# Sigmoid attention and ReGLU: part of the first queries loaded behind the first weights, and batch 1 in six bursts

One core of one Trainium2 chip. The metric is the device time of one execution in microseconds (us). The granted TensorE clock, the share of its full clock that the chip let TensorE have over a run, was 0.99 to 1.00. In lines of a profile PE is TensorE (PEld its weight loads), DVE is VectorE, ACT is ScalarE and POOL is GpSimd; what stands in brackets is idle time before the line, and what ended it.

## The reference

```python
def _attn_ref(q, k, v):                    # q, k, v: (8, 12, 448, 64) float32
    scores = (1 / sqrt(64)) * q @ k.T - log(448)
    return sigmoid(scores) @ v
def _moe_ref(x, w_gate, w_val, w_out):     # x: (3584, 768), d_ff 1536
    return (maximum(x @ w_gate, 0) * (x @ w_val)) @ w_out
```

The attention output, heads side by side, is the feed-forward input. Each of the 8 batches is one block of 448 tokens.

## The kernel before

Batch 0 is the ramp: the loads arrive while TensorE works. Its twelve heads are three groups, its queries are cut after three of seven chunks, and each of the six "slots" is one group against one half of the queries: scores, sigmoid on ScalarE, and a value product ("pv"). A feed-forward unit (`ffn_mix("f")`) is one 128-column piece of gate and value products. GpSimd issues loads that cast float32 to float16 on the way.

```python
    KCUT, QCUT = 4, 3                      # (two lines in the source)
    # first keys and queries of group 0: uncast, from SyncE and ScalarE queues; cast on VectorE, ScalarE
    make_identity(nc, ident[:])
    ...
    load(0, 0, 1, "k", KCUT)
    load(0, 1, 2, "kq")
    load(0, 2, 3, "kq")
    load(0, 0, 1, "q", QCUT)
    load_v(0)
    ...
    load_gv(0, 2)                          # gate and value weights, columns in pieces of 128
    load_gv(2, 4)
    load_gv(4, 6)
    load(1, 0, 1, "kq")
    load_gv(6, 8)
    ...
    after = {                              # (slot, unit): what TensorE does behind this unit's scores
        ...
        (0, 3): lambda: pe_transposes(0, 1, 1),
        (1, 2): lambda: pe_transposes(0, 2, 1),
        ...
        (2, 2): slots[0].pv,
        (2, 3): slots[1].pv,
        (3, 1): slots[2].pv,
        (3, 3): lambda: ffn_mix("f"),
        (4, 0): lambda: ffn_mix("f"),
        (4, 1): slots[3].pv,
        (4, 2): lambda: ffn_mix("f"),
        (5, 0): lambda: ffn_mix("f"),
        (5, 1): slots[4].pv,
        (5, 3): lambda: ffn_mix("ff"),
    }
    ...                                    # then slots[5].pv(), "the last slot's product"
        cuts = (0, 4, 7, 11, 16, 21) if b == 1 else (0, 5, 8, 13, 16, 21)   # score units of a burst
        pv_at = {3: 0, 4: 1} if b == 1 else {0: -1, 2: 0, 4: 1}
        if b == 1:
            mix = ["f" * n for n in (3, 4, 3, 3, 2)]                        # units between bursts
```

Of the kernel before, what the change touches and what calls it, by code (L numbers as in the profile page):

```python
# [17 lines left out]
def kernel(  # L18
# [10 lines left out]
    nc = tc.nc  # L29

    B, H, S, D = q.shape
    DM, DF = moe_w_gate.shape
    NPAIR = H // 2
    NG = H // 4
    P = 128
    NCH = S // 64
# [3 lines left out]
    QCUT = 3  # L40
# [32 lines left out]
    def bank(name):  # L73
        return next_ring().tile([P, 512], FP32, tag="ring", name=name)

    def bank16(name):
        return next_ring().tile([P, 1024], FP16, tag="ring", name=name)
# [5 lines left out]
    def tiles_of(b):  # L83
        if b not in in_tiles:
            in_tiles[b] = tuple(
                inp.tile([P, NPAIR, NCH * D], FP16, tag=t, name=t) for t in ("k16", "q16", "v16")
            )
        return in_tiles[b]

    def rows_of(src, b):  # L90
        return src[b].rearrange("(x r) (t c) d -> (r t) x (c d)", r=2, c=NCH)

    def load(b, g0, g1, which, c0=0):
        for nm, t16, src in zip("kq", tiles_of(b), (k, q)):
            if nm in which:
                xs = slice(2 * g0, 2 * g1)
                nc.gpsimd.dma_start(t16[:, xs, c0 * D :], rows_of(src, b)[:, xs, c0 * D :])  # L97

    def load_v(b):
        v16 = tiles_of(b)[2]  # L100
        nc.gpsimd.dma_start(v16[:, 0::2, :], rows_of(v, b)[:, 0::2, :])  # L101
        for r in range(2):
            nc.gpsimd.dma_start(  # L103
                v16[64 - 64 * r : P - 64 * r, 1::2, :], rows_of(v, b)[64 * r : 64 * r + 64, 1::2, :]
            )


    KCUT = 4
# [5 lines left out]
        first32.append(t32)  # L114
    zeros = const.tile([P, S], FP16, name="zeros")
    nc.vector.memset(zeros[:], 0.0)
    ident = const.tile([P, P], FP16, name="ident")
    make_identity(nc, ident[:])
    gate = const.tile([P, 2], FP16, name="gate")
    nc.gpsimd.tensor_copy(gate[:], zeros[:, 0:2])  # L120
    load(0, 0, 1, "k", KCUT)
    load(0, 1, 2, "kq")
    load(0, 2, 3, "kq")
    load(0, 0, 1, "q", QCUT)
    load_v(0)

# [4 lines left out]
    def load_gv(f0, f1):  # L131
        fs = slice(f0 * P, f1 * P)
        nc.gpsimd.dma_start(wg[:, :, fs], moe_w_gate[:, fs].rearrange("(c p) f -> p c f", p=P))
        nc.gpsimd.dma_start(wv[:, :, fs], moe_w_val[:, fs].rearrange("(c p) f -> p c f", p=P))

    load_gv(0, 2)
    load_gv(2, 4)
    load_gv(4, 6)
    load(1, 0, 1, "kq")
    load_gv(6, 8)  # L140
    load(1, 1, 2, "kq")
    load_gv(8, 10)
    load(1, 2, 3, "kq")
    load_gv(10, 12)
    load_v(1)

    def load_o():
# [9 lines left out]
    def keep_warm(count):  # L157
        ps = bank("warm_ps")
        for _ in range(count):
            nc.tensor.matmul(ps[:, 0:S], zeros[:, 0:P], zeros[:], start=True, stop=True)  # L160
# [19 lines left out]
    def qkT_of(b, g):  # L180
        if (b, g) not in qkT_tiles:
            qkT_tiles[(b, g)] = qkTp.tile([P, TW, P], FP16, tag="qkT", name="qkT")
        return qkT_tiles[(b, g)]

    def pe_transposes(b, g, ti, c0=0, c1=NCH):
        t16 = in_tiles[b][ti]
        qkT = qkT_of(b, g)
        trt = bank16("trt")
        for c in range(c0, c1):
            for h in range(2):  # L190
                nc.tensor.transpose(  # L191
                    trt[64 * h : 64 * h + 64, c * P : (c + 1) * P],
                    t16[:, 2 * g + h, c * D : (c + 1) * D],
                    ident[:],
                )
        nc.vector.tensor_copy(  # L196
            qkT[:, ti * NCH + c0 : ti * NCH + c1, :].rearrange("p c x -> p (c x)"),
            trt[:, c0 * P : c1 * P],
        )

    def dma_transposes(b, g):
        k16, q16, _ = in_tiles[b]
        rel = relp.tile([P, TW, P], FP16, tag="rel", name="rel")
        for ti, t16 in enumerate((k16, q16)):
            nc.vector.tensor_copy(
                rel[:, ti * NCH : (ti + 1) * NCH, :].rearrange("p c (h d) -> p h c d", h=2),
                t16[:, 2 * g : 2 * g + 2, :].rearrange("p h (c d) -> p h c d", c=NCH),
            )
        nc.sync.dma_start_transpose(
            qkT_of(b, g)[:], rel[:].rearrange("p c x -> p (c x)")  # L210
        )
# [68 lines left out]
    def qk_unit(b, g, c):  # L280
        ps = [bank("qk_ps") for _ in range(2)]
        qk(qkT_tiles[(b, g)], c, 0, NCH, lambda hh: ps[hh][:, 0:S])
        PT = PTp.tile([P, 2, 512], FP16, tag="PT", name="PT")
        for hh in range(2):
            sigmoid(PT[:, hh, 0:S], ps[hh][:, 0:S])
        PT_tiles[(b, g, c)] = PT

    def pv_group(b, g):
        pv(b, g, 0, S, [PT_tiles.pop((b, g, c))[:, :, 0:S] for c in range(NCH)])
# [69 lines left out]
    def push_gv(b, q0, qn, fs, act_relu=True):  # L359
        for f in fs:  # L360
            gv_queue.append(lambda f=f: gv(b, q0, qn, f, act_relu))

    def push_first(half, fs, act_relu=True):
        c0, c1 = HALVES[half]
        push_gv(0, 64 * c0, 64 * (c1 - c0), fs, act_relu)
# [5 lines left out]
    def ffn_mix(kinds, hooks=()):  # L371
        hooks = list(hooks)
        for left in range(len(kinds), -1, -1):
            while hooks and hooks[0][0] >= left:
                hooks.pop(0)[1]()
            if left:
                (gv_queue if kinds[len(kinds) - left] == "f" else y_queue).popleft()()
# [5 lines left out]
    nc.vector.tensor_copy(k16[:, 0:2, 0 : KCUT * D], first32[0])  # L383
    nc.scalar.copy(q16[:, 0:2, 0 : QCUT * D], first32[1])
    pe_transposes(0, 0, 0, 0, KCUT)
    keep_warm(2)
    pe_transposes(0, 0, 1, 0, QCUT)
    keep_warm(2)
    slots = [FirstSlot(g, half) for half in range(2) for g in range(NG)]
    push_first(0, range(0, 6), False)  # L390

    after = {
        (0, 0): lambda: pe_transposes(0, 0, 0, KCUT, NCH),
        (0, 1): lambda: keep_warm(2),
        (0, 2): lambda: pe_transposes(0, 1, 0),
        (0, 3): lambda: pe_transposes(0, 1, 1),
        (1, 0): lambda: keep_warm(2),
        (1, 1): lambda: pe_transposes(0, 2, 0),
        (1, 2): lambda: pe_transposes(0, 2, 1),
        (1, 3): lambda: keep_warm(2),  # L400
        (2, 0): lambda: keep_warm(2),
        (2, 1): lambda: pe_transposes(0, 0, 1, QCUT, NCH),
        (2, 2): slots[0].pv,
        (2, 3): slots[1].pv,
        (3, 1): slots[2].pv,
        (3, 3): lambda: ffn_mix("f"),
        (4, 0): lambda: ffn_mix("f"),
        (4, 1): slots[3].pv,
        (4, 2): lambda: ffn_mix("f"),
        (5, 0): lambda: ffn_mix("f"),  # L410
        (5, 1): slots[4].pv,
        (5, 3): lambda: ffn_mix("ff"),
# [15 lines left out]
    def pv_finish(b):  # L428
        pv_group(b, NG - 1)
        push_gv(b, 0, S, range(NFC))  # L430
        if b % 2:
            push_down(b // 2, range(7))
# [8 lines left out]
    def both(b, g):  # L441
        pe_transposes(b, g, 0)
        pe_transposes(b, g, 1)
# [6 lines left out]

    ffn_mix("fff", [(1, lambda: both(1, 0))])
    for b in range(1, B):
        cuts = (0, 4, 7, 11, 16, 21) if b == 1 else (0, 5, 8, 13, 16, 21)
        pv_at = {3: 0, 4: 1} if b == 1 else {0: -1, 2: 0, 4: 1}
        hooks = {}
        if b == 1:
            mix = ["f" * n for n in (3, 4, 3, 3, 2)]
            hooks = {
                1: [(1, lambda: both(1, 1))],
                2: [(1, lambda: both(1, 2))],  # L460
                3: [(1, lambda: dma_transposes(2, 0))],
                4: [(1, late_loads)],
            }
        elif b == 2:
            mix = ["fff", "fff", "ffy", "fyf", "fyf"]
        elif b % 2:
            mix = ["fyf", "fyf", "ffff", "fyf", "fyf"]
        else:
            mix = ["fff", "fyf", "fyf", "fff", "fyf"]
        for m in range(5):  # L470
            for i, (g, c) in enumerate(order[cuts[m] : cuts[m + 1]]):
                if i == (1 if b == 1 else 2) and m in pv_at:
                    if m == 0:
                        pv_finish(b - 1)
                    else:
                        pv_group(b, pv_at[m])
                qk_unit(b, g, c)
            if m >= 3 and 1 < b < B - 1:
                dma_transposes(b + 1, m - 3)
            if m == 0 and b > 1:  # L480
                dma_transposes(b, 2)
            if b == 1:
                if m == 0:
                    load(2, 0, 1, "kq")
                    load(2, 1, 2, "kq")
                    load(2, 2, 3, "kq")
            elif m == 0 and b + 1 < B:
                if b == 2:
                    hold(2, 2)
                load(b + 1, 0, 3, "kq")  # L490
                load_v(b + 1)
            ffn_mix(mix[m], hooks.get(m, ()))
# [34 lines left out]
```

## Time and profile before

| | before |
|---|---|
| time | 432.81 us (432.5 to 433.04, 4 runs) |
| TensorE busy | 422.5 of 430.9 us |
| V of batch 0 first in full use | 16.11 us |
| last slot's value product starts | 30.55 us |
| from there to the first full-width unit (batch 1's stage) | 38.11 us |
| from there to the end | 362.24 us |

### The profile page before, as it was taken

What the parts mean: (1) busy time and instruction counts of PE and PEld (TensorE: products, weight loads), DVE (VectorE), ACT (ScalarE), POOL (GpSimd) and SP (SyncE); (2) the same over time, 40 slices, a digit from 0 to 9 for tenths busy, and PEclk for the clock granted to TensorE, in tenths of its full rate; (3) what the DMA queues carried; (4) which work ended last, traced back from release to release, by engine and by line L of the source; (5) the groups of instructions that cost most, each with busy time, mean ns of one, the idle gap of its engine ahead of it and who ended that gap; (6) DMA issues with size and microseconds to landing.
All of it is one profiled execution on the core that took longest, in us unless ns stands there. A gap on an engine that the chain in (4) does not pass through costs nothing.

```text
span 430.9 us, 8612 instructions
## 1 busy us (share of the span) xinstructions
PE 422.5 (98%) x3670; PEld 235.5 (55%) x3670; DVE 130.6 (30%) x248; ACT 211.3 (49%) x451; POOL 50.5 (12%) x75
## 2 busy tenths in 40 slices
PE   8899999999999999999999999999999999999996
PEld 3587865455555455455555555455555545555563
DVE  3353344323312333222331323322332222222111
ACT  4865686645555455454554545655653545122110
POOL 8544202500120002000030000100000000000000
PEclk9999999999999999999999999999999999999999
DMA  9999946999997134944289133611333101100234
GB/s 151 199 199 200 203 74 102 198 203 204 182 157 152 13 74 82 175 90 81 44 121 172 52 79 68 122 40 39 60 73 70 37 2 38 37 2 1 47 100 110
DMA packets 69830, 43.64 MB, mean 101 GB/s; under 512 B 35104, under 2 KB 66208, under 8 KB 69792
## 3 DMA queue, kind: packets, MB, share of 16 engines
q0 software_dynamic: 31776, 23.37, 37.0%
q1 hardware_dynamic: 37664, 19.47, 22.7%
q8 instruction: 28, 0.46, 0.4%
q10 hardware_dynamic: 352, 0.26, 0.2%
q14 instruction: 10, 0.08, 0.1%
HBM read 47.19 MB, written 11.01 MB: 135 GB/s over the span
## 4 chain that ended last, share of the span: by engine, by line
PE 94%; DMA 2%; POOL 1%; DVE 1%; ACT 1%; issue 0%; ACTq 0%; POOLq 0%
PE g_ps L297 26%; PE v_ps L297 25%; PE ya L335 17%; PE qk_ps L222 9%; PE yb L335 9%; PE pv_ps L240 7%; DMA v<-in_v_dram 2%; DVE xT L168 1%; PE trt L191 1%; POOL k L97 1%; ACT PT L177 1%; POOL q L97 0%; POOL v L101 0%; POOL v L103 0%; ACT ysb L349 0%
## 5 line engine op out<-in xcount | busy, mean ns | idle before, releaser
L177 ACT ACTIVATE PT<-qk_ps 128x448 f16<-128x448 f32 (+3 forms) x318 | 150.8, 592 | 36.0 <-PE qk_ps L222 36.0
L297 PE MATMUL g_ps<-xT,wg 128*128 128x448 f16 (+2 forms) x648 | 127.7, 332 | 0.3 <-DVE xT L168 0.2
L297 PE MATMUL v_ps<-xT,wv 128*128 128x448 f16 (+2 forms) x648 | 126.8, 332 | 0.0
L315 DVE TENSOR_TENSOR hT<-gate_sb,v_ps 128x448 f16<-128x448 f32 (+2 forms) x108 | 61.1, 569 | 196.1 <-PE v_ps L297 114.8
L335 PEld LDWEIGHTS <-hT 128*128 128x128 f16 x672 | 65.7, 98 | 47.0
L306 ACT ACTIVATE gate_sb<-g_ps 128x448 f32<-128x448 f32 (+2 forms) x102 | 54.4, 545 | 75.2 <-PE g_ps L297 73.2
L297 PEld LDWEIGHTS <-wv 128*128 128x128 f16 x648 | 62.5, 98 | 47.4 <-issue 0.7
L297 PEld LDWEIGHTS <-wg 128*128 128x128 f16 x648 | 59.1, 98 | 48.7 <-issue 10.0
L335 PE MATMUL ya<-wo,hT 128*128 128x512 f16 x336 | 77.1, 379 | 0.0
L349 ACT ACTIVATE ysb<-yb 128x256 f32<-128x256 f32 x28 | 10.8, 384 | 102.1 <-PE yb L335 102.1
L222 PE MATMUL qk_ps<-qkT 64*64 64x448 f16 (+2 forms) x756 | 51.8, 336 | 2.3 <-ACT PT L177 1.1
L335 PE MATMUL yb<-wo,hT 128*128 128x256 f16 x336 | 41.3, 273 | 0.0
L240 PE MATMUL pv_ps<-PT,v 64*64 64x448 f16 (+2 forms) x756 | 36.8, 329 | 0.6 <-DMA v<-in_v_dram 0.6
L222 PEld LDWEIGHTS <-qkT 64*64 64x64 f16 x756 | 20.6, 105 | 30.1 <-issue 21.5
L168 DVE TENSOR_SCALAR xT<-pv_ps 128x448 f16<-128x448 f32 (+2 forms) x54 | 28.4, 568 | 26.2 <-PE pv_ps L240 26.2
L343 DVE TENSOR_SCALAR ysb<-ya 128x512 f32<-128x512 f32 x28 | 19.4, 692 | 55.4 <-PE ya L335 55.4
L240 PEld LDWEIGHTS <-v 64*64 64x64 f16 x756 | 21.4, 107 | 11.8 <-DMA v<-in_v_dram 0.8
L101 POOL DMA_DIRECT2D v<-in_v_dram x8 | 6.0, 747 | 172.4 <-PE qk_ps L222 172.1
L97 POOL DMA_DIRECT2D q<-in_q_dram x14 | 10.6, 759 | 9.9 <-DMA wo<-in_moe_w_out_dram 5.9
L97 POOL DMA_DIRECT2D k<-in_k_dram x14 | 10.9, 777 | 6.2 <-PE v_ps L297 1.6
L103 POOL DMA_DIRECT2D v<-in_v_dram x16 | 10.1, 635 | 2.2 <-DMA wg<-in_moe_w_gate_dram 1.3
L196 DVE COPY qkT<-trt 128x896 f16<-128x896 f16 (+2 forms) x14 | 7.5, 556 | 6.6 <-PE trt L191 6.5
(25 smaller groups left out, 54.6 us busy)
## 6 DMA issues: line engine op xcount, KB each, us to landing
out_dram<-ysb SPq DMA_DIRECT2D x54, 192.0 KB, 2.7
k<-in_k_dram POOLq DMA_DIRECT2D x5, 672.0 KB, 14.2
q<-in_q_dram POOLq DMA_DIRECT2D x5, 672.0 KB, 18.0
v<-in_v_dram POOLq DMA_DIRECT2D x8, 336.0 KB, 4.9
v<-in_v_dram POOLq DMA_DIRECT2D x16, 168.0 KB, 5.6
wg<-in_moe_w_gate_dram POOLq DMA_DIRECT2D x6, 384.0 KB, 12.7
wv<-in_moe_w_val_dram POOLq DMA_DIRECT2D x6, 384.0 KB, 12.4
k<-in_k_dram POOLq DMA_DIRECT2D x8, 224.0 KB, 10.2
```

The lines of the kernel that those rows point to most:

```text
L97: nc.gpsimd.dma_start(t16[:, xs, c0 * D :], rows_of(src, b)[:, xs, c0 * D :])
L103: nc.gpsimd.dma_start(v16[64 - 64 * r : P - 64 * r, 1::2, :], rows_of(v, b)[64 * r : 64 * r + 64, 1::2, :])
L168: nc.vector.tensor_scalar(out=xT_of(b, pr)[:, q0 : q0 + qn], in0=src, scalar1=XSCALE, scalar2=None, op0=AOP.mult,)
L177: nc.scalar.activation(PT_ap, ps_ap, AF.Sigmoid, bias=sig_bias, scale=qk_scale)
L222: nc.tensor.matmul(out_of(hh)[o : o + 64, :], qkT[rows, c, cols], qkT[rows, NCH + c0 : NCH + c1, cols], start=True, stop=True, tile_positi ...
L240: nc.tensor.matmul(ps[hh][64 * r : 64 * r + 64, 0:qn], v16[rows, 2 * g + hh, c * D : (c + 1) * D], pieces[c][rows, hh, :], start=(c == 0), ...
L297: nc.tensor.matmul(ps[-1][:, 0:qn], wt[:, dc, f * P : (f + 1) * P], xT_tiles[(b, dc)][:, q0 : q0 + qn], start=(dc == 0), stop=(dc == NDC - 1),
L306: nc.scalar.activation(gate_sb[:, 0:qn], ps[0][:, 0:qn], AF.Relu)
L315: nc.vector.tensor_tensor(out=hT_tiles[(g, f)][:, o : o + qn], in0=gate_sb[:, 0:qn], in1=ps[1][:, 0:qn], op=AOP.mult,)
L335: nc.tensor.matmul(ps[:, 0 : m1 - m0], hT_tiles[(g, f)][:, t * P : (t + 1) * P], wo[:, f, m0:m1], start=(f == 0), stop=(f == NFC - 1),)
L343: nc.vector.tensor_scalar(out=ysb[:, m0:m1], in0=ps[:], scalar1=OUT_SCALE, scalar2=None, op0=AOP.mult)
L349: nc.scalar.activation(ysb[:, m0:m1], ps[:, 0 : m1 - m0], AF.Copy, scale=OUT_SCALE)
```

## The change

The intent: the second parts of groups 1 and 2's queries aren't needed until slots 4 and 5, so they are taken out of the queue ahead of V and put behind the first weights, to let V land sooner. The first casting load moves to the head of GpSimd's work. Batch 1's scores come in six bursts of three or four units rather than five of up to five, and the later weights in pieces of three.

```diff
-    nc.gpsimd.tensor_copy(gate[:], zeros[:, 0:2])
-    load(0, 0, 1, "k", KCUT)
-    load(0, 1, 2, "kq")
-    load(0, 2, 3, "kq")
+    load(0, 0, 1, "k", KCUT)              # now ahead of make_identity
+    for g in range(1, NG):
+        load(0, g, g + 1, "k")
+        load(0, g, g + 1, "q", 0, QCUT)   # 192 columns, 384 bytes as float16
     load(0, 0, 1, "q", QCUT)
     load_v(0)
 ...
     load_gv(0, 2)
+    load(0, 1, NG, "q", QCUT)             # the query rest: 256 columns, 512 bytes
     load_gv(2, 4)
     load_gv(4, 6)
     load(1, 0, 1, "kq")
-    load_gv(6, 8)
+    load_gv(6, 9)
     load(1, 1, 2, "kq")
-    load_gv(8, 10)
+    load_gv(9, 12)
     load(1, 2, 3, "kq")
-    load_gv(10, 12)
     load_v(1)
 ...
-    keep_warm(2)                          # between the first two transposes
+    def second_queries():
+        pe_transposes(0, 1, 1, QCUT, NCH)
+        ffn_mix("f")
+        pe_transposes(0, 2, 1, QCUT, NCH)
 ...
-        (0, 3): lambda: pe_transposes(0, 1, 1),
+        (0, 3): lambda: pe_transposes(0, 1, 1, 0, QCUT),
-        (1, 2): lambda: pe_transposes(0, 2, 1),
+        (1, 2): lambda: pe_transposes(0, 2, 1, 0, QCUT),
-        (3, 3): lambda: ffn_mix("f"),
-        (4, 0): lambda: ffn_mix("f"),
+        (3, 2): lambda: ffn_mix("f"),
+        (3, 3): second_queries,
-        (4, 2): lambda: ffn_mix("f"),
+        (4, 3): lambda: ffn_mix("f"),
 ...
-        cuts = (0, 4, 7, 11, 16, 21) if b == 1 else ...
-        pv_at = {3: 0, 4: 1} if b == 1 else ...
-            mix = ["f" * n for n in (3, 4, 3, 3, 2)]
+        cuts = (0, 3, 6, 9, 13, 17, 21) if b == 1 else ...
+        pv_at = {3: 0, 5: 1} if b == 1 else ...
+            mix = ["f" * n for n in (3, 3, 3, 2, 2, 2)]
```

The transposes and loads hooked into batch 1 move with its bursts (cut here).

More of the change, by code (lines that the diff above doesn't have):

```diff
@@ L91, in rows_of, with load @@
         return src[b].rearrange("(x r) (t c) d -> (r t) x (c d)", r=2, c=NCH)
-    def load(b, g0, g1, which, c0=0):
+    def load(b, g0, g1, which, c0=0, c1=NCH):
         for nm, t16, src in zip("kq", tiles_of(b), (k, q)):
             if nm in which:
-                xs = slice(2 * g0, 2 * g1)
-                nc.gpsimd.dma_start(t16[:, xs, c0 * D :], rows_of(src, b)[:, xs, c0 * D :])
+                xs, cs = slice(2 * g0, 2 * g1), slice(c0 * D, c1 * D)
+                nc.gpsimd.dma_start(t16[:, xs, cs], rows_of(src, b)[:, xs, cs])
     def load_v(b):
@@ L452 @@
     for b in range(1, B):
-        cuts = (0, 4, 7, 11, 16, 21) if b == 1 else (0, 5, 8, 13, 16, 21)
-        pv_at = {3: 0, 4: 1} if b == 1 else {0: -1, 2: 0, 4: 1}
+        cuts = (0, 3, 6, 9, 13, 17, 21) if b == 1 else (0, 5, 8, 13, 16, 21)
+        pv_at = {3: 0, 5: 1} if b == 1 else {0: -1, 2: 0, 4: 1}
         hooks = {}
         if b == 1:
-            mix = ["f" * n for n in (3, 4, 3, 3, 2)]
+            mix = ["f" * n for n in (3, 3, 3, 2, 2, 2)]
             hooks = {
                 1: [(1, lambda: both(1, 1))],
-                2: [(1, lambda: both(1, 2))],
-                3: [(1, lambda: dma_transposes(2, 0))],
-                4: [(1, late_loads)],
+                3: [(1, lambda: both(1, 2))],
+                4: [(1, lambda: dma_transposes(2, 0))],
+                5: [(1, late_loads)],
             }
@@ L469 @@
             mix = ["fff", "fyf", "fyf", "fff", "fyf"]
-        for m in range(5):
+        for m in range(len(mix)):
             for i, (g, c) in enumerate(order[cuts[m] : cuts[m + 1]]):
-                if i == (1 if b == 1 else 2) and m in pv_at:
+                if i == 2 and m in pv_at:
                     if m == 0:
```

## The prediction

> **What bounds the kernel now.** I read the page's busy shares first, then the table of busy time by stretch, then the timeline of TensorE and of GpSimd for the first 60 us, the chain that ended last, and last the DMA view cut into short windows.
>
> ```profile
> PE 422.5 (98%) x3670; PEld 235.5 (55%) x3670; DVE 130.6 (30%) x248; ACT 211.3 (49%) x451; POOL 50.5 (12%) x75
> ```
>
> ```profile
> 0.00:20.00 20.00, 16.56 (x302) 8.88 (x302) 6.83 (x16) 12.30 (x18) 14.81 (x26) 1.00 1.14 174
> 20.00:36.00 16.00, 15.73 (x274) 12.85 (x271) 8.23 (x22) 9.01 (x12) 7.07 (x10) 1.00 1.40 198
> 36.00:70.00 34.00, 33.48 (x441) 24.71 (x439) 13.50 (x33) 27.14 (x67) 5.91 (x9) 1.00 0.90 136
> 70.00:430.90 360.90, 356.69 (x2662) 189.02 (x2660) 102.03 (x178) 162.81 (x357) 22.71 (x32) 1.00 0.51 90
> ```
>
> In the second fence the columns after the stretch and its length are the busy time of TensorE, its weight loads, VectorE, ScalarE and GpSimd, then the granted clock, the DMA share and GB/s. TensorE is the bound: from 70 us on the change touches nothing, and of the 70 us before, TensorE is idle 3.4 + 0.3 + 0.5 = 4.2 us. A part of its busy time there is filler (the warm-up matmuls; 22 of them, about 0.19 us each, so 4 us). So nothing in this change can be worth 2% (8.7 us): the question is one of a microsecond or two. The place where it is decided is the wait for V:
>
> ```profile
> 7.30 8.77 DMA v<-in_v_dram
> ...
> 16.11 0.76 PE pv_ps L240 x25
> ```
>
> ```profile
> 16.11 0.76 PE L240 MATMUL pv_ps<-PT,v 64*64 64x192 f16 x25 [0.64 <-DMA v<-in_v_dram]
> ...
> 18.93 0.41 PE L222 MATMUL qk_ps<-qkT 64*64 64x256 f16 x8 [0.39 <-ACT PT L177]
> ...
> 28.23 0.30 PE L222 MATMUL qk_ps<-qkT 64*64 64x256 f16 x4 [0.20 <-ACT PT L177]
> ```
>
> The chain of the end runs back through TensorE without a hole to 16.11 us, and there goes over into the last piece of V landing at 16.07. Only small waits for ScalarE follow. Whatever moves that landing, or puts a new wait after it, moves the end of the kernel one for one.
>
> **What the loads do.** From 2 us to 53 us the DMA never rests, so landing times follow from what stands ahead in the queue. GpSimd allows 8 loads in flight: each issue waits for the eighth before it, so its waits tell landings: V's first piece 14.0, V 16.07, the first gate weights 17.6, the first value weights 19.6, the second pair 21.6 and 23.6, the third 25.6 and 27.6.
>
> ```profile
> 14.06 0.82 POOL L134 DMA_DIRECT2D wv<-in_moe_w_val_dram  x1 [1.16 <-DMA v<-in_v_dram]
> 17.69 0.84 POOL L133 DMA_DIRECT2D wg<-in_moe_w_gate_dram  x1 [0.61 <-DMA wg<-in_moe_w_gate_dram]
> 19.68 0.82 POOL L134 DMA_DIRECT2D wv<-in_moe_w_val_dram  x1 [1.15 <-DMA wv<-in_moe_w_val_dram]
> ```
>
> What matters most is the rate by size of piece. These are the DMA view's lines for 4.0 to 4.4, 8 to 9, and 17 to 18 us:
>
> ```profile
> DMA packets 57, 0.02 MB, mean 58 GB/s; under 512 B 53, under 2 KB 57, under 8 KB 57
> ...
> DMA packets 227, 0.19 MB, mean 190 GB/s; under 512 B 15, under 2 KB 227, under 8 KB 227
> ...
> DMA packets 392, 0.20 MB, mean 197 GB/s; under 512 B 8, under 2 KB 392, under 8 KB 392
> ```
>
> At 8 us full query rows move (448 fp16, 896 bytes written): 16 engines / 227 a us = 71 ns each. At 17 us weights move (512 bytes): 41 ns each, the same 200 GB/s. At 4 us the only load in the queue is the second part of the first keys, whose pieces are 192 fp16 = 384 bytes: 16 x 400 / 57 = 112 ns each. So a 384-byte piece takes longer than an 896-byte one.
>
> **What the Trainium skill says.** "DMA: Bandwidth & Descriptors", section Specifications, gives 512 B as the smallest transfer for line rate, below which the engine does a read-modify-write. The trace agrees in direction: 58 GB/s at 384 bytes, 197 at 512. The same page, section Queues, rings and completion order, says that an engine takes turns between the queues it has work for, a packet at a time; the trace fits, since the rate at 2.8 to 3.3 us is shared by the two uncast loads. Its section Anatomy of one DMA gives about 2.0 us of fixed cost, mostly the receipt. Counting bytes at the measured rates, V's data is through at about 14.1 us and lands at 16.07, which agrees, though slow engines may be part of it.
>
> **The change, part by part.**
>
> Query loads of groups 1 and 2. The full loads (224 KB each, 1.15 us at 200 GB/s) ahead of V become 96 KB each in 384-byte pieces; the 256 KB that remain (512-byte pieces, 1.3 us) go behind the first weight pair. By bytes alone V would land 256 KB / 200 GB/s = 1.3 us sooner. By the measured piece time, each of the two takes 256 pieces x 112 ns / 16 = 1.8 us, so 0.65 us more than the full row did: V lands 1.3 us later for this part. The pieces after the rest of the queries land 1.3 + 1.3 = 2.6 us later.
>
> Casting load issued first. The second part of the first keys is issued at about 0.74 us instead of 1.49. The engines are busy with the two uncast loads until 3.7 us, so the gain is what the small pieces can use beside them, an estimate of 0.5 us. The uncast keys, now sharing each engine, land perhaps 0.5 us later than 4.04; TensorE starts later but was to wait for V at 15.07 anyway (three of V's matmuls start there), so this costs nothing at the end.
>
> So V lands at about 16.07 + 1.3 - 0.5 = 16.9, the first value weights at 20.4, the rest of the queries at 21.7, the second and third weight pairs 2.1 us later than before (25.7, 29.7).
>
> TensorE after V. Before V one pair of warm-up matmuls and 16 transposes go: free, there it waits. After V those 16 transposes come back: 2 x 0.34 us (8 take 0.34 in the timeline at 14.54), beside which the 0.42 us copies on VectorE hide behind the first feed-forward unit. From V on: value products and scores of group 2 and slot 3 at ScalarE's pace (four sigmoids of 1024 columns, 3.35 us) bring the first feed-forward unit, now one step earlier in the order, to 19.7; its value half waits to 20.4. The transposes at 21.1 wait to 21.7. Slot 4 starts at 23.45 against 21.18, with one unit (1.02 us) already done. It then has less TensorE work between its sigmoids, which costs 0.4 us of waits. The value product of the last slot, at 30.55 now, comes at 30.55 + 2.27 - 1.02 + 0.4 = 32.2: **1.65 us later**.
>
> Batch 1 in six bursts and larger weight pieces. A burst of four score units is 16 matmuls in 1.03 us; a change of kind costs about 0.1 us on each side, so one more burst costs 0.2 us. The waits that it can remove are those at 54 to 64 us: 0.03 + 0.16 + 0.33 = 0.5 us idle; I take 0.3 of it. The larger pieces change no bytes; the first of them lands 2 us later in itself, and the weights concerned have some 8 us (34.7 landed, 42.58 used). V of batch 1, about 50.5 landed and 53.91 used, is called 1.4 us sooner in the order: its slack of 3.4 falls to 3.4 - 2.1 + 1.65 - 1.4 = 1.5, enough. Net -0.1 us.
>
> Sum: +1.65 - 0.1 = +1.5 us, so **434.1 us** if small pieces cost what the one load showed.
>
> **Rivals.** First, that the 112 ns are a matter of the first casting load, not of its size: it is the only one of its kind, and the queue was just starting. For: the DMA share was under one packet an engine then, and 1.25 to 1.45 later, when packets overlap. Against: the rate is level from 3.9 to 4.7 us, and the loads behind it reach full rate while GpSimd is still issuing. Then V lands at 16.07 - 1.3 - 0.6 = 14.1, TensorE gets there at about 14, and the wait for V turns into a wait for the rest of the queries (19.0) and for ScalarE: the last slot's product comes at about 29.3, **1.2 us sooner**, and the time is 431.3. Second, that the early casting load delays the first uncast keys much more, by a microsecond, and the first slots' sigmoids (2.6 to 2.8 us a slot on ScalarE) become the bound in place of V: TensorE is then ready at about 16, still no later than V. That makes 434 to 434.5. Third, that V of batch 1 or the late weights become a new wait at 50 to 54 us: the slack above speaks against it; if the loads are later than I reckon, up to 1 us more, 435.
>
> **Range and chances.** I give the small-piece account 0.65, the first rival 0.35; 0.65 x 434.1 + 0.35 x 431.3 = 433.1. I predict 433.2, and a range from just under the first rival to the third: 430.7 to 435.2. The part touched is 70 us, of which 4.2 are idle, so a gain of 8.7 us is out of reach, and a loss of 8.7 would need a stall that nothing shows: faster by over 2% 0.01, within 2% 0.97, slower 0.02.
>
> **What would show it.** The DMA view of the changed kernel between 5 and 11 us should have two stretches near 60 GB/s with most packets under 512 B. The wait of the first value product for V should end near 16.9 (14.1 for the rival), and slot 4's first scores start near 23.4 (20.6 for the rival), with TensorE waiting for the query rest ahead of them. Waits for ScalarE in slots 4 and 5 should grow by some 0.4 us. From 70 us on, every interval should be as before, shifted by one amount. A full rate with small pieces, or an idle stretch of over a microsecond in batch 1, would prove me wrong.

## The result

433.42 us (432.83 to 433.62, 4 runs) against 432.81: a ratio of 1.0012, 95% interval 0.9995 to 1.003. Ratios here are the mean time of one kernel's fast runs over that of the other's of the same rounds, so not quite the ratio of the medians. The time was predicted to 0.2 us. That it came so close is luck: 433.2 is, to 0.1, the mean of two accounts, 434.1 and 431.3, weighted by their chances, and neither came true. The profile shows that the way there was another.

The changed kernel's page and its busy time by stretch (columns as in the prediction):

```profile
PE 423.0 (98%) x3668; PEld 235.5 (55%) x3668; DVE 130.7 (30%) x250; ACT 211.2 (49%) x451; POOL 49.5 (11%) x73
```

```profile
0.00:20.00 20.00, 17.29 (x305) 9.79 (x306) 6.55 (x18) 13.21 (x19) 15.33 (x26) 1.00 1.16 173
20.00:36.00 16.00, 15.18 (x267) 12.15 (x266) 8.34 (x22) 8.01 (x11) 5.83 (x8) 1.00 1.36 200
36.00:70.00 34.00, 33.69 (x440) 24.39 (x439) 13.64 (x33) 27.11 (x66) 5.60 (x8) 1.00 0.88 135
```

TensorE's first 20 us are 0.7 us fuller than before (17.29 against 16.56), as if something had been won; the next 16 us are 0.55 us emptier (15.18 against 15.73). This is TensorE's timeline of the changed kernel (start, length, what, count, idle time before it):

```profile
14.08 1.06 PE L240 MATMUL pv_ps<-PT,v 64*64 64x192 f16 x28
...
14.98 0.66 PE L240 MATMUL pv_ps<-PT,v 64*64 64x192 f16 x23
16.20 0.32 PE L240 MATMUL pv_ps<-PT,v 64*64 64x192 f16 x5 [0.56 <-issue]
...
18.27 0.67 PE L297 MATMUL g_ps<-xT,wg 128*128 128x192 f16 x6
...
19.60 0.41 PE L191 MATMUL trt<-ident,q 128*64 128x128 f16 x8
...
21.38 0.63 PE L222 MATMUL qk_ps<-qkT 64*64 64x256 f16 x16
...
23.90 0.30 PE L222 MATMUL qk_ps<-qkT 64*64 64x256 f16 x4 [0.50 <-ACT PT L177]
...
30.59 0.96 PE L240 MATMUL pv_ps<-PT,v 64*64 64x256 f16 x28
```

V was in use from 14.1 us and, by the chain of waits, complete by 14.4 (the fourth matmul of the product starts at 14.38), not at the predicted 16.9: 1.7 us sooner than before. The first feed-forward unit started at 18.27 us against 20.08. And yet the last slot's product came at 30.59 against 30.55. V's gain had gone within 16 us. This profile is of the fastest of the four runs (432.83 us); a second profile of the same kernel, below, is closer to the median. The dead stop of 0.56 us within the second value product waits for nothing that the profile shows, and its cause stays open. The traces hold a lead that no run tested. In all five profiles in which TensorE is early at this product (both of the changed kernel, and later rest_later, rest_first and rest_first_reordered) it halts before the same matmul, the 24th of 28, and goes on 1.4 to 1.7 us after the end of one 16 KB packet of the DMA queue that the trace calls "instruction" (here the packet moves from 13.37 to 14.54 us). In the other eight it gets to that matmul 1.76 us or more after that packet, and does not halt. So TensorE may have been waiting for its next instructions.

The same read of the DMA as in the prediction, here from 6.2 to 6.6 us of the changed kernel, where the 384-byte pieces of group 1's queries move:

```profile
DMA packets 155, 0.06 MB, mean 153 GB/s; under 512 B 144, under 2 KB 155, under 8 KB 155
```

155 packets in 0.4 us are 16 x 400 / 155 = 41 ns each on 16 engines, where the prediction had 112. The trace also has each packet's own duration: in both kernels the median 384-byte packet takes 51 ns, the 512-byte one 60 and the 896-byte one 88. Packets overlap (the engines' share in that stretch is 147% by the same view), so 41 ns apart and 51 ns long do not clash.

### The profile page after: what moved, and what is told of

The parts are those of the page before. It is cut to its first block, busy times and chain, and to the rows that moved or that the text cites. A ratio compares the mean times of both kernels' runs of the same rounds, so it can differ in the third digit from the quotient of the medians.

```text
span 431.1 us, 8609 instructions
## 1 busy us (share of the span) xinstructions
PE 423.0 (98%) x3668; PEld 235.5 (55%) x3668; DVE 130.7 (30%) x250; ACT 211.2 (49%) x451; POOL 49.5 (11%) x73
## 4 chain that ended last, share of the span: by engine, by line
PE 95%; ACT 2%; DMA 1%; DVE 1%; issue 1%; ACTq 0%
PE g_ps L297 26%; PE v_ps L297 25%; PE ya L335 17%; PE qk_ps L222 10%; PE yb L335 9%; PE pv_ps L240 7%; ACT PT L177 1%; PE trt L191 1%; PE warm_ps L160 1%; DMA qkT<-rel 1%; DVE xT L168 0%; DVE qkT L196 0%; ACT ysb L349 0%; DVE zeros L116 0%; ACTq L177 0%
## 5 line engine op out<-in xcount | busy, mean ns | idle before, releaser
L222 PEld LDWEIGHTS <-qkT 64*64 64x64 f16 x756 | 20.5, 105 | 29.1 <-issue 20.7
```

Of the source, the lines that this page charges most:

```text
L222: nc.tensor.matmul(out_of(hh)[o : o + 64, :], qkT[rows, c, cols], qkT[rows, NCH + c0 : NCH + c1, cols], start=True, stop=True, tile_positi ...
```

## The experiments

Marks of all profiles, in us. "V" is when the bulk of the first value product starts, "rest" when the transposes of the query rest start, "last" when the last slot's product starts, "batch 1" from there to the first full-width unit. The median of the kernel before, on the same chip in the same rounds, stands in brackets. Each row's marks are those of one profile. batch1_only and cast_on_act have batch 0's loads as before, so their V and "last" show how far the old marks vary: by some 0.1 us.

| kernel | V | rest | last | batch 1 | time (before) |
|---|---|---|---|---|---|
| before | 16.11 | - | 30.55 | 38.11 | 432.81 |
| changed, first profile | 14.4 | 19.60 | 30.59 | 38.23 | 433.42 (432.81) |
| after_again | 14.76 | 20.33 | 31.32 | 38.24 | 433.21 (432.39) |
| loads_only | 15.60 | 20.46 | 31.44 | 38.11 | 433.27 (432.74) |
| batch1_only | 16.13 | - | 30.58 | 38.25 | 432.74 (432.74) |
| f1_late | 15.37 | 20.00 | 30.67 | 38.25 | 433.08 (432.74) |
| f1_late_b1old | 14.83 | 19.73 | 30.39 | 38.11 | 432.55 (432.74) |
| split_inplace | 16.00 | - | 30.62 | 38.10 | 432.96 (432.39) |
| early_only | 15.74 | - | 30.37 | 38.11 | 433.00 (432.39) |
| cast_on_act | 16.23 | - | 30.68 | 38.11 | 433.35 (432.39) |
| rest_later | 14.58 | 23.93 | 36.30 | 38.11 | 438.83 (432.71) |
| rest_first | 14.39 | 20.59 | 31.58 | 38.11 | 433.65 (432.71) |
| rest_first_reordered | 14.68 | 18.00 | 30.45 | 38.11 | 432.17 (432.71) |

In all thirteen profiles the time from the first full-width unit to the end is 362.2 to 362.3 us: nothing after 70 us plays a part. The 95% intervals of the times are some 0.12 to 0.18% wide on each side, 0.5 to 0.8 us, so steps under that size are read from the marks, not from the times.

### The first part alone: loads_only

```diff
 (the changed kernel, with the batch 1 plan and the weight pieces of before)
```

> The first part alone: the loads, transposes and order of batch 0 as in the changed kernel; batch 1 in five bursts and weights in pieces of two as before. Theory S (V lands 1.7 us sooner, but ScalarE stands idle for 1.5 us ahead of slot 4 because two feed-forward units come first, and then sets the pace): the last slot's value product again near 30.6 us, the kernel within 0.3 us of before. Rival B (the first part is a real gain and the six bursts take it back): 1 us or more faster than before. The small-piece account of the prediction: V after 16.5 us and the kernel 1.6 us slower.

433.27 us, ratio 1.0013 (1.0001 to 1.0025). V came 0.5 us sooner than before, not the 1.7 of the first profile, and the last slot's product 0.9 us later. So rival B, a gain in batch 0 that the bursts take back, falls: the first part alone is no gain. Theory S, as put, expected 30.6 and got 31.44: it lacks something. The line that names it, from TensorE's timeline of this kernel:

```profile
15.60 0.76 PE L241 MATMUL pv_ps<-PT,v 64*64 64x192 f16 x25 [1.11 <-DMA v<-in_v_dram]
...
20.46 0.41 PE L192 MATMUL trt<-ident,q 128*64 128x128 f16 x8 [0.29 <-DMA q<-in_q_dram]
```

TensorE waits twice now: 1.11 us for V, and then for the query rest.

### The second part alone: batch1_only

```diff
 (the kernel before, with the changed batch 1 plan and weight pieces)
```

> The second part alone: batch 0 as before, batch 1 in six bursts and the larger later weight pieces. Theory S: within 0.3 us of before, or up to 0.6 us slower, if the 0.6 us that the changed kernel's median lies over before comes from here. Rival B: 1 us or more slower than before.

432.74 us, ratio 1.0007 (0.9993 to 1.0021). The marks say it more finely: batch 1 takes 38.23 to 38.25 us in all four kernels with six bursts and 38.10 or 38.11 in all nine with five. The sixth burst with its weight pieces costs 0.13 us, and gives nothing.

### One feed-forward unit moved: f1_late and f1_late_b1old

```diff
-        pe_transposes(0, 1, 1, QCUT, NCH); ffn_mix("f"); pe_transposes(0, 2, 1, QCUT, NCH)
+        pe_transposes(0, 1, 1, QCUT, NCH); pe_transposes(0, 2, 1, QCUT, NCH)
+        (4, 0): lambda: ffn_mix("f"),
```

> The changed kernel with one move: the second feed-forward unit goes from ahead of slot 4's scores to behind their first unit, both query transposes directly one after the other. Theory S: slot 4's first sigmoid starts near 21.0 us in place of 21.9, ScalarE's idle time ahead of it falls from 1.5 to about 0.6 us, the last slot's value product comes 0.7 to 1.0 us sooner (29.6 to 29.9), and the kernel is as much faster than the changed one. Rival B or a bound by weights landing: no change within 0.3 us; if the second weight pair is late (23.7 us) it costs nothing here, since the unit that reads it stays where it is.

> The same move with batch 1 and the weight pieces as before the change. Theory S: the last slot's value product as in f1_late (29.6 to 29.9) and the kernel 0.7 to 1.2 us faster than before, so about 431.6. Rival B: slower in batch 0 is not the matter, this is then also no faster than loads_only.

433.08 us (ratio 1.0010, 0.9998 to 1.0022) and 432.55 us (0.9999, 0.9986 to 1.0012). ScalarE's idle time ahead of slot 4 fell to 0.81 and 1.08 us, from 1.53 in the first profile, 1.89 in loads_only and 2.03 in after_again. From the start of the rest's transposes to the last slot's product it is 10.67 and 10.66 us, where the changed order takes 10.99, 10.99 and 10.98 (changed, after_again, loads_only). So the order ahead of slot 4 is worth 0.33 us: ScalarE's pace is part of the loss, a third to a half of what I expected. Otherwise it is a matter of when V and the rest land: in f1_late TensorE waits 1.27 us for V and then for no load, in f1_late_b1old 0.72 us for V and 0.33 for the rest. These are f1_late's lines:

```profile
15.37 0.76 PE L240 MATMUL pv_ps<-PT,v 64*64 64x192 f16 x25 [1.27 <-DMA v<-in_v_dram]
...
20.00 0.64 PE L191 MATMUL trt<-ident,q 128*64 128x128 f16 x16
```

### Small pieces by themselves: split_inplace

```diff
-    load(0, 1, 2, "kq")
-    load(0, 2, 3, "kq")
+    for g in range(1, NG):
+        load(0, g, g + 1, "k")
+        load(0, g, g + 1, "q", 0, QCUT)
+        load(0, g, g + 1, "q", QCUT)
```

> The kernel before, with only the full query loads of groups 1 and 2 each cut into a 384-byte and a 512-byte piece at the same place of the queue: same bytes, same order, no other change. The prediction's account (112 ns a small piece): each cut load takes 1.8 + 0.66 us in place of 1.15, so V's bytes are through 2.6 us later (16.7 us against 14.1) and V lands near 18.5. Theory S (a small piece is busy 51 ns and engines overlap them, some 46 ns apart): each takes 0.74 + 0.66 us, V's bytes are through about 0.5 us later (14.6) and the kernel is about 0.5 us slower.

Counting the queue's bytes in order by the packet sizes in the trace, V's were through at 14.45 us, against 14.16 and 14.07 in the two profiles of the uncut queue (before and batch1_only). That count is rough, since the engines run out of step: V's own last packet started at 15.17, against 14.95 and 15.40. V was in use at 16.00, against 16.11 and 16.13. The account of 112 ns a piece (16.7 and 18.5 us) is wrong by a wide margin. The cost is at most the expected half microsecond.

### The early casting load: early_only

```diff
+    load(0, 0, 1, "k", KCUT)
     ident = const.tile([P, P], FP16, name="ident")
 ...
-    nc.gpsimd.tensor_copy(gate[:], zeros[:, 0:2])
-    load(0, 0, 1, "k", KCUT)
```

> The kernel before with the first casting load issued ahead of the identity matrix, and nothing else. The prediction: V 0.5 us sooner, the kernel as much faster. Rival: the queue is held up until about 5 us by something else (in the changed kernel as in the one before it moves under 100 GB/s from 4 to 5 us), so V's bytes come through less than 0.3 us sooner and the time stays within 0.3 us.

433.00 us, ratio 1.0008 (0.9994 to 1.0022). By the same count V's bytes were through at 14.42 us, no sooner than before, and its last packet started at 14.85 against 14.95. The first value product started at 15.49 us and its bulk at 15.74, with only a short wait for V. TensorE got there 0.42 us later than before (15.49 against 15.07), its first transposes of queries having moved from 5.84 to 6.25. That isn't the edit's doing: these start at 6.19 and 6.27 in split_inplace and cast_on_act too, because the eight transposes and two warm-up matmuls ahead of them took 0.64 and some 0.7 us in these three profiles, and 0.41 and 0.55 before.

The last slot's product came 0.18 us sooner; the other half of V's 0.37 was lost at the second value weights, which land at 24.26 us and hold TensorE up in slot 4. One reason that the part gives so little is on GpSimd's timeline: the load was issued at 1.24 us against 1.49, and every casting load behind it some 0.3 us later than before (V's first at 6.19 against 5.92), since making the identity matrix now stands between. So the part is worth next to nothing, and the time doesn't resolve it.

### What holds the first casting loads: cast_on_act

```diff
-    nc.vector.tensor_copy(k16[:, 0:2, 0 : KCUT * D], first32[0])
+    nc.scalar.copy(k16[:, 0:2, 0 : KCUT * D], first32[0])
```

> The kernel before with the cast of the first keys moved from VectorE to ScalarE. It asks what holds the casting loads under 100 GB/s between 3.9 and 5.1 us, where the VectorE cast (4.10 to 4.75 us) runs. If that cast holds GpSimd back from writing descriptors, the rate in that stretch at least doubles and V's bytes are through 0.3 to 0.6 us sooner; if not, the rate there stays within 20% (145 GB/s only from 5.2 us on) and V's bytes are through at 14.1 as before. In both cases the first scores start 0.2 to 0.5 us later, which V's landing hides.

Inconclusive. From 4 to 5 us the rate was 130 GB/s against 61 before, but 99 in batch1_only, whose start is that of before, and 52 to 89 in the ten others; and V's bytes were through at 14.4 us, in use at 16.23, no sooner. What slows the casting loads at 4 to 5 us, in every version, stays open.

### The changed kernel once more: after_again

> The changed kernel unchanged, beside the kernel before on this chip, for a second profile and five more rounds. Theory S: the first profile (V in use from 14.4 us) was a lucky one; here V's last piece is in use at 14.4 to 15.6 us as in the other kernels with these loads (14.83, 15.37, 15.60), and the time is 0.3 to 0.8 us over before. If V is again at 14.4 us and the time still over before, the loss is not V's landing.

433.21 us, ratio 1.0012 (1.0000 to 1.0025). Its profiled run took 433.59 us and shows what the first profile, a lucky one, hid. TensorE waits for the query rest, and the chain of waits, asked of 13 to 34 us, says the same:

```profile
20.33 0.41 PE L191 MATMUL trt<-ident,q 128*64 128x128 f16 x8 [0.43 <-DMA q<-in_q_dram]
```

```profile
10.07 10.21 DMA q<-in_q_dram
20.29 0.04 issue
20.33 0.41 PE trt L191 x8
```

Before, this chain went back from TensorE into V at 16.07 us. Now it passes V by and goes into the load of the query rest, issued at 10.07 and landing at 20.29. This is theory R, put down for the next three runs: **the wait for V has become a wait for the query rest.** The kernel before has 14.44 us from V (16.11) to the last slot's product; this one has 10.99 from the rest. It breaks even when the rest lands by 30.55 - 10.99 = 19.56 us. The rest was there at 19.60 at the latest in the first profile, which is the tie at 30.59, and came at 20.33 and 20.46 in the others. That wait is only a part of their loss of 0.8 and 0.9 us: without it (0.43 and 0.29 us) TensorE would have been there at 19.90 and 20.17, still too late. The rest of the loss is work and halts after V, the transposes among them, and in loads_only V itself, at 15.60 us.

### The rest moved either way: rest_later and rest_first

```diff
 (loads_only, rest_later)                   (loads_only, rest_first)
     load_gv(0, 2)                         +    load(0, 1, NG, "q", QCUT)
-    load(0, 1, NG, "q", QCUT)                  load_gv(0, 2)
     load_gv(2, 4)                         -    load(0, 1, NG, "q", QCUT)
+    load(0, 1, NG, "q", QCUT)                  load_gv(2, 4)
```

> loads_only with one load moved: the rest of the queries behind the second pair of weight pieces in place of the first. Theory R (the landing of the query rest has taken V's place as the wait: from the start of its transposes to the last slot's value product takes 10.99 us in both profiles of the changed kernel and 10.98 in loads_only): the rest lands 3.9 us later, near 24.2 us, the last slot's product comes at 24.2 + 11.0 = 35.2 us, or up to 0.5 us less since ScalarE has caught up, and the kernel is 3.7 to 4.6 us slower than before. Theory S alone (ScalarE's pace sets it): no more than 1 us slower than loads_only.

> loads_only with the same load moved the other way: straight behind V, ahead of the first weight pair. Theory R: no wait for the query rest any more (it lands by 17 us), but the first value weights land 1.3 us later, at 20.2 to 20.8 us, and the first feed-forward unit's value half waits for them; the last slot's product comes 11.8 us after that (0.8 us to the transposes, 11.0 from there), at 32.0 to 32.6 us, and the kernel is 1.4 to 2.1 us slower than before. Theory S alone: as loads_only, within 0.3 us.

rest_later: 438.83 us, ratio 1.0145 (1.013 to 1.0161). The rest came at 23.93 us as expected, with a wait of 4.28 us, so the landing is the bound and ScalarE's pace is not. The last slot's product came at 36.30 us, 1.1 us beyond 35.2. TensorE's clock is why:

```profile
23.93 0.41 PE L192 MATMUL trt<-ident,q 128*64 128x128 f16 x8 [4.28 <-DMA q<-in_q_dram]
24.27 1.14 PE L298 MATMUL g_ps<-xT,wg 128*128 128x192 f16 x6
```

```profile
24.00:27.00 3.00, 3.00 (x32) 2.36 (x36) 1.15 (x4) 0.00 (x0) 1.54 (x2) 0.54 1.42 199
```

Six 192-column matmuls took 1.14 us there and 0.67 elsewhere, and the granted clock (the third column from the right of the second fence) was 0.54 from 24 to 27 us. The Trainium skill, "TensorE: Matmul & The Clock Gate", Part 1, says that a window of about 3.4 us without work halves the clock; a wait of 4.28 us with a clock of 0.54 after it agrees.

rest_first: 433.65 us, ratio 1.0021 (1.0007 to 1.0034). No wait for the rest any more; the wait is for the value weights in its stead:

```profile
17.77 0.67 PE L298 MATMUL g_ps<-xT,wg 128*128 128x192 f16 x6
19.76 0.67 PE L298 MATMUL v_ps<-xT,wv 128*128 128x192 f16 x6 [1.32 <-DMA wv<-in_moe_w_val_dram]
```

From 19.76 us it took 11.82 us to the last slot's product (31.58), as put down; the weights landed 0.4 us sooner than expected, and the loss is that much less.

### The work ordered for these landings: rest_first_reordered

```diff
 (rest_first)
-        (3, 2): lambda: ffn_mix("f"),
-        (3, 3): second_queries,
+        (3, 2): lambda: pe_transposes(0, 1, 1, QCUT, NCH),
+        (3, 3): lambda: pe_transposes(0, 2, 1, QCUT, NCH),
+        (4, 0): lambda: ffn_mix("f"),
         (4, 1): slots[3].pv,
-        (4, 3): lambda: ffn_mix("f"),
+        (4, 2): lambda: ffn_mix("f"),
         (5, 0): lambda: ffn_mix("f"),
         (5, 1): slots[4].pv,
+        (5, 2): lambda: ffn_mix("f"),
```

> rest_first with the work put in the order that these landings ask for: both query transposes in slot 3, the first feed-forward unit only after slot 4's first scores, the others spread over slots 4 and 5. Theory R: TensorE then waits for neither; V in use from 14.8 to 15.6 us, ScalarE goes from slot 3 to slot 4 with under 0.5 us idle, the last slot's product comes at 29.7 to 30.4 us and the kernel is 0.2 to 0.9 us faster than before, the first of these to be so. If the first value weights (20.2 to 20.8 us) still hold TensorE up, it comes at 30.5 to 31 us and nothing is gained.

432.17 us, ratio 0.9990 (0.9977 to 1.0003). No wait for a load is left behind V, and ScalarE goes from slot 3 into slot 4 without a gap (five sigmoids from 16.58 to 21.03 us in one piece). The last slot's product came at 30.45 us, 0.1 us before that of the kernel before: just outside what was expected. It has the lowest median of all. By the two ratios to the kernel before (0.9990 against 1.0012) it is better than the changed kernel, though the two weren't run in the same rounds; that it beats the kernel before is likely but not shown, since the interval reaches over 1.

## Why the prediction was right, and where it was wrong

The time was right by luck: two terms of the sum behind 434.1 were wrong, in opposite senses, and the 431.3 of the first rival was wrong as well.

**The bound, and what can't change.** Right. Nothing after 70 us moved but by one amount; the stage of 70 us was the whole matter, and a microsecond the size of it. One reading is off: the 22 warm-up matmuls aren't 0.19 us each, since the first ten alone take 3.92 us (1.16 to 5.08).

**"By the measured piece time, each of the two takes 256 pieces x 112 ns / 16".** This step failed. The 112 ns were time passed divided by packets, in a slow stretch: the share was under one packet an engine, against 1.25 to 1.45 later, which the prediction itself names in its first rival and then sets aside. The median packet lasts 51 ns there too; a few last up to 907 (mean 89). Nor is it a matter of the first casting load, as the first rival had it, but of the time: in the changed kernel 220 of that load's 256 pieces start from 3.4 to 4.0 us, and the stretch from 4 to 5 us is as slow (66 GB/s) with 60 of its 100 packets of 896 bytes. What slows it stays open. The packets' own durations lie on one line: 51 ns at 384 bytes, 60 at 512, 88 at 896, with no step at 512. So V was predicted 0.8 us later (16.9) and came 0.5 to 1.7 us sooner (14.4 to 15.6). The sentence that the trace agrees with the skill's 512 B was wrong with it: the 58 GB/s weren't a matter of size. The reading that V's data is through at 14.1 us was the rough count of bytes; its last packet started at 14.95.

**"Casting load issued first ... an estimate of 0.5 us".** By itself it moved the last slot's product 0.18 us; V's bytes weren't sooner. The load was issued at 1.24 us in the changed kernel, not at 0.74.

**"The value product of the last slot ... 1.65 us later".** Measured: 0.04 us and 0.77 us later in two profiles. From V on, the prediction added 1.65 - 0.8 = 0.85 us of work and waits; after_again shows 16.56 us (14.76 to 31.32) where before had 14.44, so 2.1 us. About 0.7 are the 16 transposes, which the prediction had. 0.43 are the wait for the rest. About 0.4 are a stop in the second value product (0.96 us from 15.36 to 16.32, where 0.58 is usual), and 0.2 a new wait for ScalarE, in slot 4; some 0.2 more are a pause ahead of the first unit's value half, and the last 0.2 I can't place. V's sooner landing and this larger bill all but cancel.

**The wait for the rest.** The prediction had it, in its sum and in the first rival. Where it is the last wait, the product follows it: the rest at 23.93, 20.3 to 20.5 and 19.73 us puts the product at 36.30, 31.3 to 31.4 and 30.39. In f1_late V was the last wait, so the two stand within some 0.4 us of each other. Slot 4's first scores came at 21.38 and 22.11 us, between the signs given for the two accounts (23.4 and 20.6). The first rival was nearest in mechanism. Its 1.2 us sooner failed because V landed up to 1.5 us later, and the rest 0.7 to 1.5 us later, than its 14.1 and 19.0, and because the way from the rest to the product took 10.99 us where it had 10.3.

**"Net -0.1 us" for batch 1.** Measured +0.13 us: the cost of the burst was right, the waits to be removed weren't.

Delaying one load behind another while the queue is full bought nothing that these runs resolve: the same bytes stand ahead of the weights either way, and the change trades an early wait for a later one and pays the transposes after V instead of in the wait before it.

## What to carry to other kernels

When a load is put off to let another land first, ask when the put-off data is needed and when it will land at the same queue's rate; the gain is only what lies between the two. Take the cost of a small transfer from a stretch in which the queue is full, and hold it against its packets' own durations; here a slow stretch gave 112 ns for packets whose median is 51. One profile of a load-bound start is one draw: here V's use varied by 1.2 us between kernels with the same loads, more than the effect in question.

## What the Trainium skill lacked or had wrong

- "DMA: Bandwidth & Descriptors", Specifications: below 512 B a read-modify-write and no line rate, but not how much that costs. For casting loads counted by written bytes (their float32 sources are twice as long) the packets' durations show no step there: 51 ns at 384 bytes, 60 at 512, 88 at 896, one straight line of some 23 ns and 0.072 ns a byte. The rate does fall, as the page says: while moving mostly 384-byte pieces the queue made 153 GB/s against 197, where the durations alone would give some 174 (an estimate: 197 x 384 / 51 x 60 / 512).
- Same page, Anatomy of one DMA: a fixed cost of about 2.0 us, mostly the receipt. From the start of V's last packet to V in use it was 0.6 to 1.5 us in the twelve profiles in which TensorE waits for V, 1.16 in the kernel before. The part behind the last byte is thus under 2.0 us here, and not constant.
